# Window attention and a Mish feed-forward on one core: every engine's order from a list scheduler inside the kernel

## Chip, core and metric

The kernel runs on one core of a Trainium2 chip. TensorE (PE) multiplies matrices into PSUM, of which this kernel uses eight banks, VectorE (DVE), ScalarE (ACT) and GpSimd (POOL) work on tiles, and SyncE (SP) issues the transfers. The program gives each engine one queue of instructions; one that waits for another engine holds up those that stand behind it. The metric is the device time in microseconds of one execution.

## Reference

Windowed causal attention (window 64, 8 sequences of 576 tokens, 8 heads of 64), whose output is the input of a feed-forward 512 -> 2048 -> 512 with the Mish function between:

```python
scores = scale * np.matmul(q, k.transpose(0, 1, 3, 2))
scores = np.where(mask, scores, -1000000000.0)
attn = np.exp(scores - np.max(scores, axis=-1, keepdims=True))
attn = attn / (np.sum(attn, axis=-1, keepdims=True) + 1e-09)
x = np.matmul(attn, v)                      # then heads side by side: 4608 x 512
h = x @ w_in
g = h * np.tanh(np.log1p(np.exp(h)))        # Mish
out = g @ w_out
```

All is float32. The kernel multiplies in the format fp32r: each operand of the feed-forward is split into a high and a low part, and three products (high x high, high x low, low x high) are summed.

## The kernel before

**Tiling.** The 4608 tokens are cut into 12 chunks of 384. For each chunk, attention runs in four units, one for each pair of heads, and gives one of four 128-row blocks of x^T. Then the feed-forward runs in 16 steps, one for each block of 128 hidden values; step f of chunk c is written (c,f) here. A step is H: 12 matmuls into one of two h banks (four blocks of x, three products each), then Mish on ACT (L220), a high part gh (ACT L222 in chunk 0, POOL L224 later), a low part gl (POOL L225), and, two steps later (LAG = 2), A: 9 matmuls into the three accumulator banks of the chunk. The last A of a chunk is followed by a copy of each bank and a store (L241 to L244).

**A unit of attention** is S: scores (24 small matmuls on the profile); for each of six 128 x 128 tiles a masked row minimum on DVE (L149) and an exponential on ACT (L152); a normalisation on DVE (L156 to L162); a transposition; V: the product with v (24 small matmuls); and the split of x into xh (ACT L204) and xl (DVE L205). In chunks 0 to 3 the transposition is T: six PE transposes and two copies out of PSUM (L183, L184); from chunk 4 on DVE transposes 32 x 32 blocks and 12 small transfers move them (L172, L177).

**Weights.** The 16 blocks of weights arrive as 64-bit floats, one 1 MB transfer each (L251), and are converted in the kernel: absolute value on ACT (L261), four operations on DVE (L262, L264, L265, L266), the high part on ACT (L270), the low part on DVE (L271). A load waits until the weights three blocks earlier are converted (the lines on `used`). Weight f is needed by H and A of (0,f), and after that by every chunk.

**Order.** Chunk 0 runs eight steps alone, then its steps alternate with those of chunk 1, whose step f stands beside step f + 8 of chunk 0 (HEAD = 8). The four units of chunk 1 are spread over the first eight steps, those of chunk 2 over the last steps of chunk 1, and the units of every later chunk over the steps of the chunk before it. Up to the start of chunk 2 the tile framework's scheduler decides in which order each engine gets these instructions; it sees `high_priority` marks only. From chunk 2 on, `in_order` ties PE to the order of the program text. PSUM banks come from three pools (accumulators 3, h 2, attention 3), whose tiles are handed out as the text asks for them.

Of the kernel before, what the change touches and what calls it, by code (L numbers as in the profile page):

```python
# [13 lines left out]
I64 = mybir.dt.int64  # L14
# [8 lines left out]
SOON = 400  # L23
WP = 512


@with_exitstack
def tile_window_attn_mish_ffn(
# [13 lines left out]
    NC_ = NPAIR  # L42
# [6 lines left out]
    LAG = 2  # L49

    const = ctx.enter_context(tc.tile_pool(name="const", bufs=1))
    xp = ctx.enter_context(tc.tile_pool(name="xp", bufs=1))
    ap_ = ctx.enter_context(tc.tile_pool(name="ap_", bufs=2))
    mp = ctx.enter_context(tc.tile_pool(name="mp", bufs=2))
    ps_acc = ctx.enter_context(tc.tile_pool(name="ps_acc", bufs=1, space=bass.MemoryType.PSUM))
    ps_h = ctx.enter_context(tc.tile_pool(name="ps_h", bufs=2, space=bass.MemoryType.PSUM))
    ps_at = ctx.enter_context(tc.tile_pool(name="ps_at", bufs=3, space=bass.MemoryType.PSUM))

    nc.scalar.preload_act_table_set("exp_and_others")
    ident = const.tile([P, P], F32, name="ident")  # L60
    make_identity(nc, ident)

# [19 lines left out]
    ws = []  # L82


    pTs = [const.tile([P, P // 32, HM, 32], F32, name=f"pT{i}") for i in range(2)]
    for t in pTs:
        nc.gpsimd.memset(t, 0.0)
    pTs = itertools.cycle(pTs)


    order = []
    ordered = []

    def pe(*args, **kw):
        order.append(nc.tensor.matmul(*args, **kw).ins)  # L95
# [11 lines left out]
    def load_qk(c, p):  # L110
        q_t = ap_.tile([P, CH], F32, name="q_t")
        k_t = ap_.tile([P, CH + BLK], F32, name="k_t", bufs=2)
        parts = NM if c == 0 and p < 1 else 1
        for i in range(parts):
            a, b = i * CH // parts, (i + 1) * CH // parts
            nc.sync.dma_start(q_t[:, a:b], qT[p, :, c * CH + a:c * CH + b])
            a, b = a + BLK * (i > 0), b + BLK
            nc.sync.dma_start(k_t[:, a:b], kT[p, :, c * CH + a:c * CH + b])
        return q_t, k_t

    def load_v(c, p):

        v_t = ap_.tile([P, NB, P], F32, name="v_t", bufs=2)
        src = vN[p, c * CH:, :]
        nc.sync.dma_start(v_t, bass.AP(tensor=vN.tensor, offset=src.offset,
                                       ap=[[P, P], [BLK * P, NB], [1, P]]))
        return v_t

    def att_scores(c, p, tiles):
        q_t, k_t = tiles  # L130
        s_ps = [bank(c, p, "s_ps").rearrange("p (m k) -> p m k", k=P) for _ in range(2)]
        pr = ap_.tile([P, HM, P], F32, name="pr", bufs=2)
        mx = ap_.tile([P, HM], F32, name="mx", bufs=3)
        sm = ap_.tile([P, HM], F32, name="sm", bufs=3)
        for m in range(NM):
            for par, h in ((0, 0), (1, 1), (1, 0), (0, 1)):
                n = 2 * m + par
                rows = slice(h * BLK, (h + 1) * BLK)
                pe(s_ps[h][par * BLK:(par + 1) * BLK, m, :],
                   q_t[rows, n * BLK:(n + 1) * BLK], k_t[rows, n * BLK:n * BLK + P],  # L140
                                 start=True, stop=True)
        for h in range(2):
            js = slice(h * NM, (h + 1) * NM)
            for m in range(NM):
                first = [(c * NB + 2 * m + par) % blocks_per_seq == 0 for par in range(2)]
                mk = firsts[first.index(True)] if any(first) else mask
                j = h * NM + m

                nc.vector.tensor_tensor_reduce(  # L149
                    out=pr[:, j, :], in0=s_ps[h][:, m, :], in1=mk,  # L150
                    op0=ALU.add, op1=ALU.min, scale=-0.125, scalar=3.0e38, accum_out=mx[:, j:j + 1])
                nc.scalar.activation(pr[:, j, :], pr[:, j, :], AF.Exp, bias=mx[:, j:j + 1], scale=-1.0,  # L152
                                     accum_out=sm[:, j:j + 1])
            if c == 0:

                nc.vector.tensor_scalar(sm[:, js], sm[:, js], 1e-9, None, ALU.add)  # L156
                nc.vector.reciprocal(sm[:, js], sm[:, js])
                nc.vector.tensor_tensor(pr[:, js, :], pr[:, js, :], sm[:, js].unsqueeze(2).to_broadcast([P, NM, P]), ALU.mult)
        if c > 0:
            nc.vector.tensor_scalar(sm, sm, 1e-9, None, ALU.add)  # L160
            nc.vector.reciprocal(sm, sm)
            nc.vector.tensor_tensor(pr, pr, sm.unsqueeze(2).to_broadcast([P, HM, P]), ALU.mult)  # L162
        return pr

    def att_transpose(c, p, pr):
        pT = next(pTs)
        if c > 3:


            moved = []  # L170
            tr = ap_.tile([P, P // 32, HM, 32], F32, name="tr", tag="pr", bufs=2)
            nc.vector.transpose(tr.rearrange("p k j i -> p j k i"),  # L172
                                pr.rearrange("p j (k i) -> p j k i", i=32))
            for r in range(0, P, 32):
                for k in range(0, P, 32):
                    if 0 <= k - r % BLK <= BLK:
                        moved.append(nc.sync.dma_start(pT[k:k + 32, r // 32, :, :], tr[r:r + 32, k // 32, :, :]))  # L177
            return pT, moved
        for h in range(2):
            t_ps = (bank(c, p, "t_ps") if c else ps_h.tile([P, CH], F32, name="t_ps", tag="h_ps")  # L180
                    ).rearrange("p (m k) -> p m k", k=P)
            for m in range(NM):
                nc.tensor.transpose(t_ps[:, m, :], pr[:, h * NM + m, :], ident)  # L183
            (nc.scalar.copy if h == 0 or c == 1 else nc.vector.tensor_copy)(  # L184
                pT[:, :, h * NM:(h + 1) * NM, :].rearrange("p r m i -> p m r i"),
                t_ps.rearrange("p m (r i) -> p m r i", i=32))
        return pT, []

    def att_values(c, p, v_t, pT, x):
        pT, moved = pT  # L190
        xh, xl = x
        o_ps = bank(c, p, "o_ps")
        for n in range(NB):
            m, par = n // 2, n % 2
            for h in range(2):
# [237 lines left out]
```

## Time and profile before

| | |
|---|---|
| median of 3 runs | 979.98 us (979.28 to 980.83) |
| the profiled execution | 979.27 us, its span 977.5 us |
| mean granted TensorE clock | 0.976 |
| busy share of the span: PE / DVE / ACT / POOL | 95% / 28% / 43% / 30% |
| chain that ended last | PE 87%, DVE 7%, ACT 3% |
| matmuls of H: 2304, of A: 1728 | 81% of the chain is theirs (40% and 39% as the page rounds them) |

The span is the time from the first to the last instruction; the execution's own time is 1.77 us longer. The shares are averages over two quite different parts: the first eighth, in which weights are converted and PE has gaps, and the rest, in which PE has none. They must be read apart, which the prediction does.

### The profile page before, as it was taken

The page shows a single profiled execution, that of the slowest core. Times are in us where ns is not written, and L with a number is a line of the kernel's source. Part 1 is how long each engine was busy: PE and PEld are TensorE (multiplying, and loading weights), DVE is VectorE, ACT ScalarE, POOL GpSimd, SP SyncE. Part 2 cuts the span into 40 slices and gives each one's busy share as a digit, 9 for nine tenths or more (in the row PEclk, how much of TensorE's full clock was granted, in tenths as well). Part 3 has the DMA queues.
Part 4 walks back from the last instruction along what each step waited for, and adds up shares of the span by engine and source line. Part 5 has one row for each costly group of instructions (what it writes and reads, how often), then busy time and mean ns, then how long its engine had stood idle before and what let it go on. Part 6 is the DMA issues. An engine that isn't in the chain of part 4 may idle for free.

```text
span 977.5 us, 16844 instructions
## 1 busy us (share of the span) xinstructions
PE 929.9 (95%) x6432; PEld 821.7 (84%) x6432; DVE 276.3 (28%) x916; ACT 417.8 (43%) x1004; POOL 292.8 (30%) x385
## 2 busy tenths in 40 slices
PE   4698599998999999999999999999999999999998
PEld 2586399887888898888889888898888889889997
DVE  6988800122231321221221221221221221220000
ACT  5689511553553533533533443443443353451111
POOL 1023033231223233333333333333323323323332
PEclk9599699998999999999999999999999999999999
DMA  9655200122121311311311312322222221210000
GB/s 312 229 193 199 95 1 1 50 68 83 52 68 47 113 53 53 113 51 54 112 51 55 110 51 56 101 60 56 90 71 56 85 78 54 84 30 13 33 1 33
DMA packets 78033, 76.09 MB, mean 78 GB/s; under 512 B 9344, under 2 KB 71296, under 8 KB 75904
## 3 DMA queue, kind: packets, MB, share of 16 engines
q1 hardware_dynamic: 77952, 75.01, 24.5%
q8 instruction: 51, 0.84, 0.4%
q14 instruction: 30, 0.25, 0.1%
HBM read 56.10 MB, written 9.44 MB: 67 GB/s over the span
## 4 chain that ended last, share of the span: by engine, by line
PE 87%; DVE 7%; ACT 3%; issue 1%; DMA 1%; SPq 1%; ACTq 0%
PE h_ps L95 40%; PE acc L95 39%; PE o_ps L95 4%; PE s_ps L95 4%; DVE w L271 1%; DVE wa L265 1%; DVE wa L266 1%; DMA st<-w 1%; DVE wa L262 1%; DVE wa L264 1%; ACT wa L261 1%; ACT pr L152 1%; DVE pr L149 1%; PE t_ps L183 1%; ACT L220 1%
## 5 line engine op out<-in xcount | busy, mean ns | idle before, releaser
L95 PE MATMUL h_ps<-xh,w 128*128 128x384 f32 x1536 | 431.1, 341 | 3.7 <-ACT xh L204 2.7
L95 PE MATMUL acc<-w,gh 128*128 128x512 f32 x1152 | 363.5, 397 | 1.5 <-ACT gh L222 1.5
L95 PEld LDWEIGHTS h_ps<-xh,w 128*128 128x128 f32 x1536 | 284.2, 190 | 13.9 <-ACT xh L204 3.3
L220 ACT ACTIVATE t<-h_ps 128x384 f32<-128x384 f32 x192 | 94.0, 491 | 440.4 <-PE h_ps L95 439.7
L95 PE MATMUL h_ps<-xl,w 128*128 128x384 f32 x768 | 260.8, 340 | 2.9 <-DVE xl L205 2.9
L224 POOL TENSOR_SCALAR gh<-t 128x384 fp32r<-128x384 f32 x176 | 90.3, 513 | 568.6 <-ACT t L220 566.1
L95 PEld LDWEIGHTS acc<-w,gh 128*128 128x128 f32 x1152 | 211.9, 188 | 39.7 <-issue 6.3
L225 POOL TENSOR_TENSOR gl<-t,gh 128x384 fp32r<-128x384 f32 x192 | 198.4, 1034 | 106.9 <-ACT gh L222 92.2
L95 PE MATMUL acc<-w,gl 128*128 128x512 f32 x576 | 224.5, 391 | 0.6 <-POOL gl L225 0.6
L95 PEld LDWEIGHTS h_ps<-xl,w 128*128 128x128 f32 x768 | 145.8, 190 | 11.5 <-DVE xl L205 3.9
L205 DVE TENSOR_TENSOR xl<-o_ps,xh 128x384 fp32r<-128x384 f32 x48 | 26.7, 556 | 379.4 <-ACT xh L204 379.4
L95 PEld LDWEIGHTS acc<-w,gl 128*128 128x128 f32 x576 | 108.2, 188 | 25.1 <-POOL gl L225 1.0
L152 ACT ACTIVATE pr<-pr,mx 128x128 f32<-128x128 f32 x288 | 112.1, 391 | 14.8 <-DVE mx L149 14.3
L149 DVE CUSTOM_DVE_ANT_0 pr<-s_ps,mask 128x128 f32<-128x128 f32 x288 | 64.6, 285 | 30.8 <-PE s_ps L95 30.8
L220 ACT ACT_TABLE_LOAD x48 | 61.6, 1283 | 12.7 <-PE h_ps L95 12.4
L152 ACT ACT_TABLE_LOAD x42 | 53.9, 1283 | 28.9 <-DVE mx L149 28.7
L95 PEld LDWEIGHTS o_ps<-pT,v_t 128*64 128x64 f32 x1152 | 43.7, 150 | 24.3 <-issue 11.2
L95 PE MATMUL o_ps<-pT,v_t 128*64 128x64 f32 x1152 | 51.9, 240 | 9.8 <-DVE pT L184 4.7
L95 PE MATMUL s_ps<-k_t,q_t 64*64 64x128 f32 x1152 | 50.8, 293 | 4.0 <-DMA k_t<-kT 4.0
L152 ACT ACTIVATION_READ_ACCUMULATOR pr<-pr,mx 128x1 f32 x288 | 54.0, 187 | 0.0
L243 DVE COPY o<-acc 128x512 f32<-128x512 f32 x12 | 8.3, 692 | 149.2 <-PE acc L95 148.8
L95 PEld LDWEIGHTS s_ps<-k_t,q_t 64*64 64x64 f32 x1152 | 36.1, 140 | 11.3 <-DMA q_t<-qT 3.9
(36 smaller groups left out, 343.9 us busy)
## 6 DMA issues: line engine op xcount, KB each, us to landing
v_t<-vN SPq DMA_DIRECT2D x48, 384.0 KB, 3.7
st<-w SPq DMA_DIRECT2D x16, 1024.0 KB, 5.1
k_t<-kT SPq DMA_DIRECT2D x47, 224.0 KB, 3.8
out<-o SPq DMA_DIRECT2D x36, 256.0 KB, 2.1
pT<-tr SPq DMA_DIRECT2D x384, 24.0 KB, 1.8
q_t<-qT SPq DMA_DIRECT2D x47, 192.0 KB, 3.7
q_t<-qT SPq DMA_DIRECT2D x3, 64.0 KB, 2.0
k_t<-kT SPq DMA_DIRECT2D x2, 64.0 KB, 2.1
```

The lines of the kernel that those rows point to most:

```text
L95: order.append(nc.tensor.matmul(*args, **kw).ins)
L149: nc.vector.tensor_tensor_reduce(out=pr[:, j, :], in0=s_ps[h][:, m, :], in1=mk, op0=ALU.add, op1=ALU.min, scale=-0.125, scalar=3.0e38, acc ...
L152: nc.scalar.activation(pr[:, j, :], pr[:, j, :], AF.Exp, bias=mx[:, j:j + 1], scale=-1.0, accum_out=sm[:, j:j + 1])
L183: nc.tensor.transpose(t_ps[:, m, :], pr[:, h * NM + m, :], ident)
L205: nc.vector.tensor_tensor(xl[:, p, :], o_ps, xh[:, p, :].bitcast(F32), ALU.subtract)
L220: nc.scalar.activation(t, h_ps, AF.Mish)
L224: nc.gpsimd.tensor_scalar(gh, t, 1.0, 0.0, ALU.mult, ALU.add)
L225: nc.gpsimd.tensor_tensor(gl, t, gh.bitcast(F32), ALU.subtract)
L261: nc.scalar.activation(af, hi.bitcast(F32), AF.Abs)
L262: nc.vector.tensor_scalar(af, af, BIG, TINY, ALU.min, ALU.max)
L264: nc.vector.tensor_scalar(a, a, 3, 0x3FFFFFFF, ALU.logical_shift_left, ALU.bitwise_and)
L265: nc.vector.scalar_tensor_tensor(a, hi, 0xC0000000, a, ALU.bitwise_and, ALU.bitwise_or)
```

## The change

All pools and the framework's scheduling go. Every tile and PSUM bank is named by hand (rings of fixed buffers; accumulators A, attention banks B, two h banks H), every piece of work becomes a task with an engine, a cost, a rank and the tasks that it waits for, and a list scheduler in the kernel (`Plan.order`) plays the program once with the table of costs and issues the tasks in the order in which it started them. Wherever an engine is free it takes, of the tasks that are ready at that moment, the one of lowest rank (a change of ACT's function table adds 50 to a rank).

What else differs:

- Chunk 1 follows chunk 0 by seven steps (TRAIL = 7), and the ranks put its first unit (unit 4) next to the units of chunk 0.
- Weights get ranks behind the units of chunk 0. A load waits for the conversion two blocks earlier, not three. From block 5 on the absolute value is taken on DVE.
- In chunks 0 and 1, gh is made on ACT and gl on DVE; POOL makes both from chunk 2 on.
- Accumulators of chunk 0 are A, of chunk 1 B, of later ones A; units of chunk 2 use A after chunk 0 has been stored. They run during the last seven steps of chunk 1.
- Chunk 3 is transposed by DVE and transfers, as later chunks were.
- q and k of the first unit come as one transfer each (before: three each), k on ACT's queue.
- DVE copies two of the three output banks, ACT one (before: the other way round).
- H of the first two steps of chunk 0 is cut into four tasks, so that it can begin before the last block of x; the first and last A of a chunk are cut by bank.

```diff
+COST = {
+    "h": 2.08, "hcc": 0.52, "acc": 2.06, "acc1": 0.687, "scores": 0.85, "values": 0.88, "tr": 0.65,
...
+SLOW_UNTIL, SLOW = 70.0, 1.2
...
+            now = [rt for rt in ready[e] if rt[0] <= at + 1e-6]
+            pick = min(now, key=key)
...
+            free[e] = t.start + t.cost * (SLOW if e == "PE" and at < SLOW_UNTIL else 1.0)
...
+        return sorted(self.tasks, key=lambda t: (t.start, t.n))
...
+    ctx.enter_context(tc.manual_schedule())
...
+        pace = used[f - 2:f - 1] if f > 1 else []
...
+        load = add("SP", "issue", load, writes=[buf], rank=rank - 1.5, size=P * 2 * WP * 8,
+                   after=pace or [units[f].scored])
+        if on_act:
+            x = add("ACT", "abs", lambda: nc.scalar.activation(af, words[1].bitcast(F32), AF.Abs),
+                    reads=[buf], writes=[abuf], rank=rank, table="exp")
+        else:
+            x = add("DVE", "absv", lambda: nc.vector.tensor_scalar(a, words[1], 0x7FFFFFFF, None, ALU.bitwise_and),
+                    reads=[buf], writes=[abuf], rank=rank)
...
+        queue = nc.scalar if c == 0 and p == 0 else nc.sync
...
+        post = -1 + rank * 1e-3 if c < 2 else rank - 6
...
+        if c < 2:
+            add("ACT", "gh", lambda: nc.scalar.copy(gh, t), reads=[tb], writes=[ghb], rank=post)
+            add("DVE", "gl", lambda: nc.vector.tensor_tensor(gl, t, gh.bitcast(F32), ALU.subtract),
+                reads=[tb, ghb], writes=[glb], rank=post)
...
+    RANK_U = [0, 1, 4, 6, 2, 21, 34, 36]
...
+    RANK_U += [140 + i for i in range(4)]
...
+    def r_ffn(c, f):
+        return 100 + 10 * f + (TRAIL * 10 + 5 if c else 0)
...
+    seq = sorted([(f + TRAIL * c + 0.5 * c, c, f) for c in range(2) for f in range(NF)])
+    for n, (_, c, f) in enumerate(seq):
+        ffn_in(c, f, r_ffn(c, f), False, c == 0 and f < 2)
...
+    tasks = plan.order()
...
+    for t in tasks:
+        t.emit()
```

What this does to the order shows at three places.

**DVE, the last unit of chunk 0.** Before, ahead of `xl`, the low part of the last block of x of chunk 0 (the last row below), DVE's order holds six weights all but finished; this is the end of that stretch. L149 is the masked minimum of unit 4, `wa` the weights under conversion, `w` their low part, `st` the loaded words.

```order
L149 ISA pr,mx<-s_ps,mask 128x128
L149 ISA mx 128x1
L264 TENSOR_SCALAR wa<-wa 128x1024
L271 TENSOR_TENSOR w<-wa,w 128x2x512
L265 SCALAR_TENSOR_TENSOR wa<-st,wa 128x1024
L160 TENSOR_SCALAR sm<-sm 128x6
L205 TENSOR_TENSOR xl_233<-o_ps,xh_232 128x384
```

Now the same instruction (L398, the last row) has only the first weight finished ahead of it and the second begun.

```order
L327 TENSOR_TENSOR pr_95<-pr_95,sm_101 128x768
L248 TENSOR_SCALAR wa_119<-wa_119 128x1024
L353 COPY pT_104<-acc_125 128x3x4x32
L266 TENSOR_TENSOR w<-wa_118,w 128x2x512
L249 TENSOR_SCALAR wa_119<-wa_119 128x1024
L314 ISA pr_96,mx_99<-at_129,mask 128x128
L314 ISA mx_99 128x1
L251 SCALAR_TENSOR_TENSOR wa_119<-st,wa_119 128x1024
L398 TENSOR_TENSOR xl_121<-acc_126,xh_120 128x384
```

In all, before holds 28 operations on weights ahead of that row (six each of L262, L264 and L265, five each of L266 and L271), now eight (two each of L248, L249, L251, one each of L256, L266); the first row of the second fence is the normalisation of unit 4, which before comes later.

**PE, the first unit of chunk 1.** `acc`, `at`, `h` are banks; `k_t,q_t` marks scores, `pT,v_t` values, `xh` and `xl` H, `gh` and `gl` A. Before, the values of unit 4 stand inside H of (0,4), with the scores of unit 5 between them:

```order
L95 MATMUL h_ps<-xh_232,w 128x384
L95 MATMUL o_ps<-pT_102,v_t 64x64
L95 MATMUL s_ps<-k_t,q_t 64x128 x12
L95 MATMUL o_ps<-pT_102,v_t 64x64 x11
L95 MATMUL h_ps<-xh_232,w 128x384
```

Now they stand right behind the first two banks of A of (0,0), ahead of H of (0,1), which begins in the last row:

```order
L295 MATMUL at_129<-k_t_91,q_t_89 64x128
L451 MATMUL acc_124<-w,gh_109 128x512 x2
L451 MATMUL acc_124<-w,gl_112 128x512
L451 MATMUL acc_125<-w,gh_109 128x512 x2
L451 MATMUL acc_125<-w,gl_112 128x512
L384 MATMUL at_127<-pT_103,v_t_93 64x64 x12
L409 MATMUL h_130<-xh_120,w 128x384
```

The scores in the first of these rows are already those of unit 6, which before come behind H of (0,8). All four units of chunk 1 are now done ahead of H of (0,6); before, the values of the last one come behind H of (0,9).

**ACT, the units of chunk 2.** Before, exponentials (L152) and Mish (L220) share ACT in groups of three to six and one or two:

```order
L152 ACT_TABLE_LOAD
L152 ACTIVATE pr,sm<-pr,mx 128x128 x6
L204 CAST xh_1681<-o_ps 128x384
L220 ACT_TABLE_LOAD
L220 ACTIVATE t<-h_ps 128x384 x2
L184 COPY pT_102<-t_ps 128x3x4x32
```

Now (L318 exponential, L424 Mish, L426 gh):

```order
L424 ACT_TABLE_LOAD
L424 ACTIVATE t_106<-h_130 128x384
L318 ACT_TABLE_LOAD
L318 ACTIVATE pr_95,sm_101<-pr_95,mx_98 128x128
L426 CAST gh_111<-t_106 128x384
L353 COPY pT_104<-acc_126 128x3x4x32
L318 ACTIVATE pr_95,sm_101<-pr_95,mx_98 128x128 x2
L424 ACT_TABLE_LOAD
L424 ACTIVATE t_107<-h_131 128x384
```

Each Mish now stands alone between two table loads, and gh is ACT's too: from the first exponential of the four units to the Mish behind the last there are 12 loads, before ten.

More of the change, by code (lines that the diff above doesn't have):

```diff
@@ L121, in load_v @@
-    def load_v(c, p):
-        v_t = ap_.tile([P, NB, P], F32, name="v_t", bufs=2)
-        src = vN[p, c * CH:, :]
[L125 to L134, printed above, removed]
+    ident = const.tile([P, P], F32, name="ident")
@@ L138, in att_scores @@
                 rows = slice(h * BLK, (h + 1) * BLK)
-                pe(s_ps[h][par * BLK:(par + 1) * BLK, m, :],
-                   q_t[rows, n * BLK:(n + 1) * BLK], k_t[rows, n * BLK:n * BLK + P],
+                nc.tensor.matmul(u.s[h][0][par * BLK:(par + 1) * BLK, m * P:(m + 1) * P],
+                                 u.q[0][rows, n * BLK:(n + 1) * BLK], u.k[0][rows, n * BLK:n * BLK + P],
                                  start=True, stop=True)
-        for h in range(2):
[L143 to L158, printed above, removed]
@@ L193, in att_values, with emit_values @@
+    def emit_values(u):
+        v_t, pT, o_ps = u.v[0], u.pT[0], u.o[0]
         for n in range(NB):
@@ L196, in att_values @@
                 rows = slice(h * BLK, (h + 1) * BLK)
-                pe(o_ps[rows, n * BLK:(n + 1) * BLK], v_t[:, n, rows],
-                   pT[:, 2 * par:2 * par + 2, h * NM + m, :], start=True, stop=True)
-                for d in moved:
-                    tc.add_manual_dep(order[-1], d.ins.name, SYNC, reason="values in one piece")
-                moved = []
-        with tc.high_priority(offset=SOON):
-            nc.scalar.copy(xh[:, p, :], o_ps)
-            nc.vector.tensor_tensor(xl[:, p, :], o_ps, xh[:, p, :].bitcast(F32), ALU.subtract)
@@ L395, in tile_window_attn_mish_ffn, with values @@
-    while pend:
-        with in_order():
-            flush()
+                mm = nc.tensor.matmul(o_ps[rows, n * BLK:(n + 1) * BLK], v_t[:, n, rows],
+                                      pT[:, 2 * par:2 * par + 2, h * NM + m, :], start=True, stop=True)
+                for d in u.moved:
+                    tc.add_manual_dep(mm.ins, d.ins.name, SYNC, reason="values in one piece")
+                u.moved = []
+    def values(u, rank, chain):
+        add("PE", "values", lambda: emit_values(u), reads=[u.v[1], u.pT[1]], writes=[u.o[1]], rank=rank, chain=chain)
@@ new lines, in tile_window_attn_mish_ffn, with bank, tail, front @@
+    rot = [0]
+    def bank(pool):
+        rot[0] += 1
+        return pool[(rot[0] - 1) % 3]
+    def tail(i):
+        u, r = units[i], RANK_U[i]
+        if i >= 4:
+            pool = B if i < 8 else A
+            u.t = [bank(pool), bank(pool)]
+            u.o = bank(pool)
+        turn_pe(u, r, ("ACT", "ACT") if 4 <= i < 8 else ("ACT", "DVE"), False)
+        values(u, r, False)
+        refill_v(i)
+        x_parts(u, r)
+    def front(i):
+        u, r = units[i], RANK_U[i]
+        if i >= 4:
+            pool = B if i < 8 else A
+            u.s = [bank(pool), bank(pool)]
+        scores(u, r, False)
+        refill_qk(i)
+        softmax(u, r, i < 4)
@@ new lines, in tile_window_attn_mish_ffn @@
+    for n, (c, f) in enumerate(steps):
+        r = 1000 + 10 * n
+        ffn_in(c, f, r, True, False)
+        for kind, i in sorted(runs.get(n, []), key=lambda x: x[0], reverse=True):
+            u = units[i]
+            if kind == "s":
+                u.s, u.o = B[:2], B[2]
+                scores(u, r, True)
+                refill_qk(i)
+                softmax(u, r - 4, False)
+                turn_dma(u, r - 4)
+            else:
+                values(u, r, True)
+                refill_v(i)
+                x_parts(u, r - 5)
+        if n >= LAG:
+            ffn_out(*steps[n - LAG], r + 15, True)
```

577 lines of the change are left out of this document (357 added, 220 removed).

## Prediction

> **What bounds the kernel now.** The page's slices and a table of windows come first: they say where PE, which carries 87% of the chain, is not at work. The columns of a window are its length, then busy time and count for PE, PEld (weight load), DVE, ACT and POOL, the granted clock, the DMA share and GB/s.
>
> ```profile
> PE   4698599998999999999999999999999999999998
> DVE  6988800122231321221221221221221221220000
> PEclk9599699998999999999999999999999999999999
> 0.00:49.10 49.10, 27.19 (x260) 20.08 (x260) 41.56 (x122) 29.75 (x82) 4.12 (x17) 0.76 0.79 271
> 49.10:121.60 72.50, 54.95 (x385) 45.37 (x385) 64.66 (x103) 58.11 (x101) 13.36 (x9) 0.90 0.47 163
> 121.60:223.10 101.50, 101.47 (x627) 89.60 (x627) 12.88 (x63) 37.88 (x88) 31.37 (x39) 0.99 0.09 29
> 223.10:235.50 12.40, 9.07 (x53) 8.20 (x52) 2.87 (x6) 4.25 (x11) 0.15 (x1) 0.72 0.33 98
> 235.50:977.50 742.00, 737.17 (x5110) 658.45 (x5109) 154.38 (x623) 287.80 (x725) 243.76 (x320) 1.00 0.21 63
> ```
>
> Up to 121.6 us PE is busy 27.2 + 55.0 = 82.1 us and idle 39.5, while DVE is busy 106.2: softmax and weights on DVE bound this stretch. From 121.6 to 223.1 PE has no gap; from 223.1 to 235.5 it loses 3.3 us waiting for the last unit of chunk 2; from there it is busy 737.2 of 742.0 us, the rest being the last copy and store. So the change can win only ahead of 235.5. The pitch of PE's work, from the chain (start, length, what) and the timeline (the same, by runs of instructions):
>
> ```profile
> 160.71 2.11 PE h_ps L95 x12
> 164.87 2.11 PE h_ps L95 x12
> 334.52 0.92 PE L95 MATMUL o_ps<-pT,v_t 128*64 128x64 f32 x24
> 353.05 0.92 PE L95 MATMUL o_ps<-pT,v_t 128*64 128x64 f32 x24
> 205.62 0.87 PE L183 MATMUL t_ps<-ident,pr 128*128 128x128 f32 x6
> 206.42 0.65 PE L95 MATMUL s_ps<-k_t,q_t 64*64 64x128 f32 x6
> ```
>
> H to H is 4.16 us, a **step** (H 2.1, A 2.06). Two V in a row start 18.53 us apart with four steps and one S + V between, so S + V cost 18.53 - 16.64 = 1.89. T costs 0.80. The first two chunks' 32 steps and the first three chunks' 12 units are then 133.1 + 12 x 2.69 = 165.4 us of PE at full rate. Before spends 235.5 on them.
>
> **The part behind chunk 1.** At 235.5 before still has A of (1,15) to do and has done H of (2,0); these cancel. The time behind chunk 1's last A is then 742.0 us, less the four T of chunk 3, which leave PE for DVE and transfers: 742.0 - 3.2 = 738.8. I cost nothing for their new path: scores and values of a chunk-3 unit stand four steps apart, as in later chunks, whose window shows no gap. The last copy on DVE instead of ACT is worth a tenth. With T1 for the end of chunk 1's last A, span = T1 + 738.8.
>
> **When the feed-forward gets under way.** Before, `xl` of the last block of x of chunk 0 releases PE. Below it stand DVE operations by start and length; the step from one start to the next is what an operation costs the queue.
>
> ```profile
> 48.54 0.55 DVE L205 TENSOR_TENSOR xl<-o_ps,xh 128x384 fp32r<-128x384 f32 x1
> 49.14 0.45 PE L95 MATMUL h_ps<-xl,w 128*128 128x384 f32 x1 [0.82 <-DVE xl L205]
> 49.00 1.22 DVE L266 SCALAR_TENSOR_TENSOR wa<-st,wa 128x1024 uint32<-128x1024 uint32 x1
> 50.14 0.69 DVE L262 TENSOR_SCALAR wa<-wa 128x1024 f32<-128x1024 f32 x1
> 50.74 0.18 DVE L161 RECIPROCAL sm<-sm 128x6 f32<-128x6 f32 x1
> 50.86 0.69 DVE L264 TENSOR_SCALAR wa<-wa 128x1024 uint32<-128x1024 uint32 x1
> 51.47 0.95 DVE L162 TENSOR_TENSOR pr<-pr,sm 128x768 f32<-128x768 f32 x1
> 52.34 1.22 DVE L271 TENSOR_TENSOR w<-wa,w 128x1024 fp32r<-128x1024 f32 x1
> 61.66 1.22 DVE L271 TENSOR_TENSOR w<-wa,w 128x1024 fp32r<-128x1024 f32 x1
> 62.79 1.22 DVE L266 SCALAR_TENSOR_TENSOR wa<-st,wa 128x1024 uint32<-128x1024 uint32 x1
> 12.53 0.28 DVE L149 CUSTOM_DVE_ANT_0 pr<-s_ps,mask 128x128 f32<-128x128 f32 x1
> 12.74 0.28 DVE L149 CUSTOM_DVE_ANT_0 pr<-s_ps,mask 128x128 f32<-128x128 f32 x1
> ```
>
> A short weight operation (L262, L264) costs 0.61, a long one (L265, L266, L271) 1.13, a six-tile normalisation 0.87, `xl` 0.46, a masked minimum 0.21. By the order, before has 12 short and 16 long weight operations ahead of this `xl`, 25.4 us; now 4 and 4, 7.0: 18.4 us less. Unit 4's normalisation with its two small operations (0.87 + 0.3) and one more minimum (0.2) now stand ahead: +1.4. DVE was busy 41.6 of the 49.1 us, so nearly all of this counts: 49.1 - 18.4 + 1.4 = 32.1.
>
> ```profile
> q_t<-qT SPq DMA_DIRECT2D x47, 192.0 KB, 3.7
> q_t<-qT SPq DMA_DIRECT2D x3, 64.0 KB, 2.0
> st<-w SPq DMA_DIRECT2D x16, 1024.0 KB, 5.1
> ```
>
> The first q lands whole after 3.7 us, not in thirds after 2.0, and k is issued behind ACT's first table load; the thirds overlapped with scores, so I take 1.2 us of the 1.7: 33.3. Last, weights no longer fill DVE's waits in the softmax of chunk 0. If all of them stay filled, 33.3 holds or 32 with an unchanged first load; if the 7.5 us in which DVE idled there come once more, 41. I take a third of that, **36**, since scores of units 4 and 5 still fill some.
>
> By then PE has done units 0 to 3 (10.8), scores of units 4 and 5 and half a T (2.2), and three quarters of H of (0,0) (1.6): 165.4 - 14.6 = **150.8** remain.
>
> **What holds PE up after that.** Three terms.
>
> ```profile
> 229.25 4.14 PE h_ps L95 x12
> 18.04 1.22 DVE L271 TENSOR_TENSOR w<-wa,w 128x1024 fp32r<-128x1024 f32 x1
> 118.69 1.23 DVE L271 TENSOR_TENSOR w<-wa,w 128x1024 fp32r<-128x1024 f32 x1 [1.17 <-ACT w L270]
> L270 ACT CAST w<-wa 128x1024 fp32r<-128x1024 f32 x16 | 16.7, 1046 | 8.1 <-DVE wa L266 8.0
> 17.00 1.56 PE L95 MATMUL s_ps<-k_t,q_t 64*64 64x128 f32 x24
> ```
>
> (a) Clock: after a gap H took 4.14 us instead of 2.11. One such start is **2** us (0 if the units keep the clock up, 4 if a second gap follows).
>
> (b) Weights. DVE's share of one weight is now 3 short operations (the absolute value, taken like L264, for which before has no row on DVE) and 3 long, 5.2 us, plus two gl. Before has no gl on DVE; the nearest row is `xl`, the same subtraction at 0.46. That makes 6.1 us for each weight against 8.3 for two steps of PE, so once both chunks run PE is the slower, and the later gl and absolute values cost nothing: PE hides them, and would pay about 2 us for each 2 us by which DVE went over 8.3. Before the units of chunk 1 are done it is the other way round: (0,1) to (0,5) need five weights (26 us), three units (six minima, normalisation, `xl`, 2.9 us each) and four gl (2), 37 us of DVE, against five steps and three units of PE, 29 us. DVE does some of this before 36, the first weights being under way. I take **5** us of waiting, between 2 (one Mish, gh, gl chain ahead of A of (0,0)) and 12, most of the 17.5 us that PE idled in before's second window. A load now waits for the weight two back, and behind it on SP stand loads of q, k and v; landing takes 5.1 us, less than the 6.1 of one weight, so nothing comes late for it.
>
> (c) The units of chunk 2, in the last seven steps of chunk 1, share ACT with Mish and gh.
>
> ```profile
> 190.21 0.49 ACT L220 ACTIVATE t<-h_ps 128x384 f32<-128x384 f32 x1
> 190.72 1.28 ACT L152 ACT_TABLE_LOAD   x1
> 192.01 0.40 ACT L152 ACTIVATE pr<-pr,mx 128x128 f32<-128x128 f32 x1
> L152 ACT ACTIVATE pr<-pr,mx 128x128 f32<-128x128 f32 x24 | 9.3, 390 | 3.4 <-DVE mx L149 3.4
> 221.41 0.87 PE L95 MATMUL s_ps<-k_t,q_t 64*64 64x128 f32 x12
> 226.22 0.85 PE L183 MATMUL t_ps<-ident,pr 128*128 128x128 f32 x6 [3.08 <-DVE pr L162]
> ```
>
> Twelve loads are 15.4 us, 24 exponentials 9.4, six Mish and six gh (taken alike) 6, eight copies out of PSUM (taken alike) 4: 35 us of ACT beside 6 H, 6.7 A and four units on PE, 37 us. ACT just fits. Between the last scores and their transposes before had 226.2 - 222.3 = 3.9 us of chain, 3.1 of it idle on PE; now A, T, H, V and A stand there, 8 us, which covers it. I take **3** us, between 0 and 8 (a Mish held up by a load and a few exponentials in each of four units).
>
> The Trainium skill, "ScalarE: Activation LUTs", section "What ACT_TABLE_LOAD costs", puts a switch at about 1283 ns of load and 1380 ns of drain. The trace agrees with the first and shows no second: Mish ends at 190.70, the load runs 190.72 to 192.00, the exponential starts at 192.01. By that section ACT would need 16.6 us more for the twelve.
>
> **Sum.** T1 = 36 + 150.8 + 2 + 5 + 3 = 196.8; span 935.6; the profiled execution lies 1.77 us above its span and 0.7 below the median of the runs: 938.1 against 979.98. All low ends give T1 = 184.8 and 926, all high ends 215.8 and 957.
>
> **Rivals.**
> 1. *The fixed order waits where the list did not expect it.* The planner puts scores in this stretch at 0.85 x 1.2 = 1.02 us; at low clock before shows 24 of them in 1.56 us (17.00 above). If what then stands first in a queue is late, all behind it is. If PE idles as it did from 49.1 to 121.6 (17.5 us instead of 5) and x comes 2 us later, T1 = 211.3, time 952.6. For it: DVE's stretch up to (0,5) has no slack. Against: PE and DVE had such orders before, and the gap came from chunk 1's x arriving after the weights.
> 2. *ACT limits the end of chunk 1.* If a switch held ACT for a load and as long again, about 16 us more, T1 would grow by 13: 951. The rows above speak against it.
> 3. *Slower: weights one after another.* Should a load and its conversion not overlap, a weight takes 5.1 + 5.2 + 1.0 (high part on ACT) = 11.3 us. With the first at 31 the last comes at 31 + 15 x 11.3 = 200.5; behind it stand half a step, eight steps and chunk 2's units, 46 us: T1 = 246.5, time 987.8. It turns slower than before at T1 = 238.7, 10.8 us for each weight. Against: before's first and last L271 are 100.6 us apart, 6.7 for each of 15, with units between, and two loads may be under way.
> 4. *More than forecast*, below 927: DVE's waits all filled and weights just in time.
>
> **How the numbers follow.** Forecast 0.64, rival 1 0.20, rival 2 0.03, rival 3 0.05, rival 4 0.08. Predicted is the forecast, 938.1. From 927 to 956 lie the forecast with nearly all its bounds and rivals 1 and 2. A measurement of this kernel tells about 0.2% from no change: slower is rival 3 alone (0.05), same a chance meeting near its turning point (0.01), faster the rest (0.94).
>
> **What would show it.** Right: the last `xl` of chunk 0 near 36 us; PE's idle time up to its last A of chunk 1 mostly ahead of 36; no PE gap from about 70 us to 160; chunk 1's last A near 197; 739 us from there to the end; no T in chunk 3. Wrong: `xl` beyond 41 (DVE's waits were hidden by weights), H waiting for L266 in step after step (weights set the pace), H or A waiting for ACT from 160 on, or gaps behind chunk 2's start, which the whole sum takes as unchanged.

## The result and the profile after

The changed kernel takes 939.51 us (median of four runs, 937.72 to 940.72), against 979.63 of the kernel before in runs on the same chip: a ratio of 0.959 (95% interval 0.957 to 0.961), 40 us less. The execution that was profiled took 938.71 us, 1.8 above its span of 936.9.

Of the page of the changed kernel, the rows of busy tenths in 40 slices:

```profile
PE   6789999999999999999999999999999999999998
DVE  5999952433232122212222123113212222220000
PEclk9799999999999999999999999999999999999999
```

Before, the slices of PE dip in the first five and again at the tenth. Now only the first three (and the last) are under 9, and the granted clock is under 9 tenths in one slice instead of three. The table of windows, with the columns of before (length, busy time and count of PE, PEld, DVE, ACT and POOL, clock, DMA share, GB/s):

```profile
0.00:33.90 33.90, 22.70 (x273) 17.48 (x274) 24.35 (x106) 21.18 (x76) 4.22 (x17) 0.92 0.81 256
33.90:80.00 46.10, 40.53 (x312) 33.88 (x311) 45.89 (x94) 36.70 (x76) 0.00 (x0) 0.95 0.58 201
80.00:157.30 77.30, 77.30 (x388) 69.66 (x386) 52.31 (x67) 28.92 (x48) 0.00 (x0) 1.00 0.28 101
157.30:194.80 37.50, 37.50 (x353) 32.33 (x353) 18.41 (x75) 33.32 (x80) 0.00 (x0) 1.00 0.30 91
194.80:936.90 742.10, 738.04 (x5089) 656.22 (x5087) 163.49 (x634) 281.17 (x710) 243.94 (x320) 1.00 0.22 65
```

Up to chunk 1's last A at 194.8 us PE is idle 11.2 + 5.6 = 16.8 us; before, up to 235.5, it was 21.9 + 17.6 + 0 + 3.3 = 42.8. That is 26.0 us less idle time. The same work also kept PE busy for 178.0 us instead of 192.7, at a clock of 0.92 and 0.95 in the first two windows, where before had 0.76, 0.90 and 0.72 in three of its four. 26.0 + 14.7 = 40.7 us is what T1, the end of chunk 1's last A, has gained. Nothing was gained behind it: that part takes 742.1 us, where 738.8 was forecast and before had 742.0.

The two rows that mark T1 and the release of the feed-forward, from the timelines of DVE and PE (start, length, what):

```profile
33.42 0.55 DVE L398 TENSOR_TENSOR xl<-acc,xh 128x384 fp32r<-128x384 f32 x1
194.53 0.39 PE L451 MATMUL at<-w,gl 128*128 128x512 f32 x1
194.76 0.34 PE L409 MATMUL h<-xh,w 128*128 128x384 f32 x1
```

The last `xl` of chunk 0 ends at 34.0 us, and the first H of chunk 2 starts at 194.76, right behind the last A of chunk 1. What PE waited for between 34 and 157 us, the four longest groups (waits by line: total, times, longest):

```profile
PE at L348 <- DVE mx L314: 2.1, 2, 1.1
PE acc L451 <- DVE gl L427: 1.5, 2, 0.8
PE at L348 <- DVE pr L327: 0.8, 1, 0.8
PE at L295 <- ACT pT L353: 0.6, 1, 0.6
```

All of it lies ahead of 73 us. Of the 5.6 us that PE waits, 4.4 are for DVE, which is busy 45.9 of the 46.1 us from 33.9 to 80.

### The profile page after: what moved, and what is told of

It is laid out like the page before. It is cut to its first block, busy times and chain, and to the rows that moved or that the text cites. A ratio compares the mean times of both kernels' runs of the same rounds, so it can differ in the third digit from the quotient of the medians.

```text
span 936.9 us, 16721 instructions
## 1 busy us (share of the span) xinstructions
PE 916.1 (98%) x6408; PEld 809.6 (86%) x6408; DVE 304.4 (32%) x971; ACT 401.3 (43%) x989; POOL 248.2 (26%) x337
## 4 chain that ended last, share of the span: by engine, by line
PE 92%; DVE 5%; DMA 1%; issue 0%; ACT 0%; SPq 0%
PE h L409 42%; PE acc L451 39%; PE at L451 4%; PE at L384 3%; PE at L295 3%; DVE wa L251 1%; DVE wa L256 1%; DMA st<-w 1%; DVE w L266 1%; DVE pr L314 1%; DVE pr L327 1%; PE acc L295 1%; DVE wa L248 0%; DMA k_t<-kT 0%; PE acc L384 0%
## 5 line engine op out<-in xcount | busy, mean ns | idle before, releaser
L409 PE MATMUL h<-xh,w 128*128 128x384 f32 x1536 | 426.2, 338 | 0.0
L409 PEld LDWEIGHTS h<-xh,w 128*128 128x128 f32 x1536 | 281.7, 188 | 8.4 <-issue 0.3
L424 ACT ACTIVATE t<-h 128x384 f32<-128x384 f32 x192 | 94.2, 491 | 430.4 <-PE h L409 429.8
L409 PE MATMUL h<-xl,w 128*128 128x384 f32 x768 | 258.5, 337 | 0.0
L432 POOL TENSOR_TENSOR gl<-t,gh 128x384 fp32r<-128x384 f32 x160 | 162.0, 1013 | 13.3
L409 PEld LDWEIGHTS h<-xl,w 128*128 128x128 f32 x768 | 144.6, 188 | 7.8
L398 DVE TENSOR_TENSOR xl<-at,xh 128x384 fp32r<-128x384 f32 x41 | 22.8, 557 | 335.7 <-ACT xh L397 335.7
L318 ACT ACTIVATE pr<-pr,mx 128x128 f32<-128x128 f32 x288 | 112.2, 391 | 9.5 <-DVE mx L314 8.9
L314 DVE CUSTOM_DVE_ANT_0 pr<-at,mask 128x128 f32<-128x128 f32 x252 | 57.0, 285 | 22.2 <-PE at L295 22.2
L318 ACT ACTIVATION_READ_ACCUMULATOR pr<-pr,mx 128x1 f32 x288 | 54.0, 187 | 0.0
L327 DVE TENSOR_TENSOR pr<-pr,sm 128x768 f32<-128x768 f32 (+1 forms) x52 | 46.4, 895 | 1.4
L295 PE MATMUL at<-k_t,q_t 64*64 64x128 f32 x1008 | 40.2, 287 | 2.4 <-DMA k_t<-kT 1.1
L384 PE MATMUL at<-pT,v_t 128*64 128x64 f32 x984 | 38.0, 226 | 1.0 <-ACT pT L353 0.4
```

The lines of the kernel that those rows point to most:

```text
L295: nc.tensor.matmul(u.s[h][0][par * BLK:(par + 1) * BLK, m * P:(m + 1) * P], u.q[0][rows, n * BLK:(n + 1) * BLK], u.k[0][rows, n * BLK:n * ...
L314: x = add("DVE", "ttr", lambda: nc.vector.tensor_tensor_reduce(out=pr[:, j, :], in0=u.s[h][0][:, m * P:(m + 1) * P], in1=mk, op0=ALU.add, ...
L318: return add("ACT", "exp", lambda: nc.scalar.activation(pr[:, j, :], pr[:, j, :], AF.Exp, bias=mx[:, j:j + 1], scale=-1.0, accum_out=sm[:, ...
L327: return add("DVE", "norm3" if n == NM else "norm6", lambda: nc.vector.tensor_tensor(pr[:, js, :], pr[:, js, :], sm[:, js].unsqueeze(2).to ...
L384: mm = nc.tensor.matmul(o_ps[rows, n * BLK:(n + 1) * BLK], v_t[:, n, rows], pT[:, 2 * par:2 * par + 2, h * NM + m, :], start=True, stop=True)
L398: add("DVE", "xl", lambda: nc.vector.tensor_tensor(xl[:, p, :], o_ps[:, :CH], xh[:, p, :].bitcast(F32), ALU.subtract), reads=[u.o[1]], wri ...
```

## The experiments

Two questions were open. **Which part of the change carries the gain?** The theory was the prediction's: the weights now stand behind the softmax of chunk 0 on DVE, x is ready early, and once both chunks run PE has no gap. The rivals were the early unit 4, gl's move from POOL to DVE, and the distance of seven steps. **Why are there 742.1 us behind T1 and not 738.8?** No PE wait is there and no T in chunk 3, but two V in a row stand 18.62 us apart in the changed kernel, where before had 18.53:

```profile
482.22 0.92 PE L384 MATMUL at<-pT,v_t 128*64 128x64 f32 x24
500.84 0.92 PE L384 MATMUL at<-pT,v_t 128*64 128x64 f32 x24
```

### Both kernels again, on one chip

No edit.

> The kernel before, unchanged, profiled on the same chip as the changed one. The part behind chunk 1's last A took 742.1 us in the changed kernel where 738.8 was forecast, since a step of its steady part took 4.185 us against 4.16 before. If the two kernels' code or tiles make the difference, two V in a row with four steps and one S between them stand 18.53 us apart here, and 18.62 in the changed kernel on the same chip. If it was the chip or the execution, both show the same pitch, 18.53 or 18.62.

> The changed kernel, unchanged, on the same chip as the kernel before. Kernel as the cause: a pitch of 18.62 us (two V in a row) and 742 us from the last A of chunk 1 to the end. Chip or execution as the cause: the pitch of the kernel before on this chip, and 739 us. Last xl of chunk 0 ends at 34 us and chunk 1's last A at 195 us either way.

On the same chip, in one execution each, the kernel before took 981.1 us with its V at 483.97 and 502.50 us, 18.53 apart. The changed kernel took 940.16, with V at 483.58 and 502.20, 18.62 apart, and 741.9 us behind T1. So the longer step belongs to the kernel, not to the chip. T1 came at 196.4 us in this execution instead of 194.8: between these two executions of one kernel the start differs by 1.6 us, the steady part by 0.2.

### The tiles in other places

```
...
-    gh_ring = Ring("gh", 3, [P, CH], F32R)
+    gh_ring = Ring("gh", 3, [P, CH], F32R, space=mp)
...
-    xs = [[const.tile([P, NPAIR, CH], F32R, name=f"x{n}{i}") for n in "hl"] for i in range(2)]
+    xs = [[xp.tile([P, NPAIR, CH], F32R, name=f"x{n}{i}") for n in "hl"] for i in range(2)]
```

> The changed kernel with its SBUF tiles in four pools in the order of the kernel before (constants and weights, then x, then q, k, v, pr, then the feed-forward's), so that x, gh, gl and the weights lie where they lay or near it; no instruction is another. If the places of the tiles make a step 0.025 us longer, the pitch falls from 18.62 to 18.53 us and the time by 3 us to 936.5. If something else does, the pitch stays at 18.62 and the time at 939.5 within 1.

Measured: 935.56 us (ratio 0.954, interval 0.953 to 0.956), V 18.53 us apart, 738.8 us behind T1. No instruction was changed, and the missing 3.3 us are back: the places of the tiles had cost them. What about the places it was, the next three runs show.

### 64 bytes

In the changed kernel all tiles lie in one pool in the order of their declaration. The six tiles `mx` and `sm` take 32 bytes each, 192 together, so all tiles behind them (pT, t, gh, gl, o, wa, x, w) start 64 bytes off a multiple of 128. In the kernel before, w and x lie in pools ahead of `mx` and `sm`, at a multiple of 128, while gh and gl lie behind them, 64 off.

```
+    const.tile([P, 16], F32, name="pad")
     xs = [[const.tile([P, NPAIR, CH], F32R, name=f"x{n}{i}") for n in "hl"] for i in range(2)]
```

> The changed kernel with 64 bytes of each partition left empty ahead of x: x and the weights move up by 64 bytes and then start at a multiple of 128, as they did before and in the run with the tiles in four pools; in the changed kernel they start 64 bytes off one. Nothing else moves. If the 64 bytes make a step 0.025 us longer, two V in a row stand 18.53 us apart, 738.8 us lie behind chunk 1's last A, and the time falls by 3 to 4 us to about 936. If it is which tiles lie beside which, the pitch stays at 18.62 and the time within 1 us of 940.

Measured: 935.94 us (ratio 0.955, interval 0.953 to 0.956), 738.9 us behind T1, and in the timeline of this run V stand 18.53 us apart:

```profile
481.03 0.92 PE L385 MATMUL at<-pT,v_t 128*64 128x64 f32 x24
499.56 0.92 PE L385 MATMUL at<-pT,v_t 128*64 128x64 f32 x24
```

> The changed kernel with t, gh, gl, o and wa in a pool behind the weights, so that x and the weights move down by 29,696 bytes but still start 64 bytes off a multiple of 128, while Mish's and POOL's tiles now lie on the other side of the weights, as before. If the 64 bytes are the cause, the pitch stays at 18.62 us and 742 us lie behind chunk 1's last A. If the neighbourhood of the tiles is the cause, 18.53 and 738.8.

The edit of this run is the one on gh_ring above, for t, gh, gl, o and wa alone. Measured: 939.08 us (one execution), V at 482.49 and 501.11, 18.62 apart, 741.9 us behind T1. The neighbourhood of the tiles does nothing, as expected if the 64 bytes are the cause. The last run of this question moved the same empty tile one place up, ahead of pT:

```
+    const.tile([P, 16], F32, name="pad")
     pT_ring = Ring("pT", 2, [P, P // 32, HM, 32])
```

> The changed kernel with the 64 empty bytes one place earlier, ahead of pT: not only x and the weights, but also t, gh, gl, o and wa then start at a multiple of 128 (in both kernels and in every run so far they start 64 off one). If the 64 bytes cost PE on any operand, the nine weight loads of gh and gl in each step gain what the ones of x and w gained: up to 0.025 us a step, 160 steps behind chunk 1's last A and 32 ahead, 4 to 5 us, time 931 to 932. If DVE's and ACT's operations on wa and t also go faster, the long weight operation falls below 1.22 us and T1 falls too. If only x or the weights count, the pitch is that of the run with the 64 bytes ahead of x, 18.53 us, and the time 936 within 1.

Measured: 940.51 us (ratio 0.960, interval 0.958 to 0.961), V at 484.84 and 503.46, 18.62 apart. **This expectation failed, and with it the rule behind the earlier two**: w and x start at a multiple of 128 here, and the step is long all the same. What the runs have in common shows in A's matmuls from 300 to 900 us (by one line of the program: count, then shortest/median/longest in ns). The changed kernel, where w and gl both start 64 bytes off:

```profile
L451 PE MATMUL acc<-w,gl x391: 389/397/398, 299.6 to 899.3; 128*128 128x512 f32 x196
```

The run with 64 bytes ahead of x (w at a multiple of 128, gl 64 off):

```profile
L452 PE MATMUL acc<-w,gl x392: 388/388/398, 302.2 to 899.5; 128*128 128x512 f32 x196
```

The run with t, gh, gl, o and wa last (both 64 off):

```profile
L452 PE MATMUL acc<-w,gl x391: 389/397/398, 299.9 to 899.5; 128*128 128x512 f32 x196
```

The run with all at a multiple of 128:

```profile
L452 PE MATMUL acc<-w,gl x390: 389/397/398, 300.9 to 897.7; 128*128 128x512 f32 x195
```

The median is 397 ns where gl, the operand that is loaded, and w, the one that streams, start at the same place modulo 128, and 388 where they start 64 bytes apart. The run with other places (w at a multiple of 128, gl 64 off) has 388 too, and the kernel before (the same) 389. Matmuls overlap, so what a step costs is read from one start to the next, worked out from the same traces (medians): the nine matmuls of an A take 2.081 us in the changed kernel, in the run with t, gh, gl, o and wa last and in the run with all at a multiple of 128, and 2.061 in the other three; the twelve of an H take 2.105 or 2.106 in all six. That is 20 ns a step, 0.08 us in four steps and 3.2 us in the 160 behind T1, as measured (742.1 against 738.9). The medians leave out that about three H in ten differ as well (2.110 us against 2.084). The longer gl matmul stays so from 85 to 155 us, where POOL is idle (means of 396 in the changed kernel, 388 with the 64 bytes), so POOL is not the other party. In all six placements x lies with w, and t, gh, o and wa lie with gl, modulo 128: that it is gl and w, and not another pair of these tiles, follows only from the matmul in which it shows. The Trainium skill, "SBUF — State Buffer", section "Who interferes with whom", gives PE two independent read ports, one for the operand that streams and one for the loaded one, and says that PE waits on nobody; here the measured times differ with the place of these two operands. Why the matmul with gl is slowed and those with gh are not, no run tells.

### The weights first

```
-    RANK_W = [15, 18, 5, 30, 16, 14] + [55 + 5 * i for i in range(10)]
+    RANK_W = [-4, -3, -2, -1, 16, 14] + [55 + 5 * i for i in range(10)]
```

> The changed kernel with the first four weights ranked ahead of the softmax of chunk 0, as they stood before: 13 short and 15 long weight operations (24.9 us of DVE) ahead of the last xl of chunk 0 instead of 4 and 4 (7.0). Theory (x of chunk 0 is early because the weights stand behind it): this xl moves from 34 us to between 42 (weights fill the 9.6 us in which DVE idled) and 52 (all 17.9 count), about 47 us; PE's 5.6 us of waits behind it go in part, since the weights are ready then, so T1 rises by 7 to 13 us, to about 204, and the time to about 949. Rival (the gain comes from unit 4 being early and from gl off POOL, not from the weights' place): xl may move but the time stays within 3 us of 939.5.

Measured: 952.4 us (ratio 0.971, interval 0.970 to 0.973), 12.9 us above the changed kernel. From DVE's timeline and the windows:

```profile
50.10 0.55 DVE L398 TENSOR_TENSOR xl<-acc,xh 128x384 fp32r<-128x384 f32 x1
0.00:50.60 50.60, 27.62 (x286) 20.75 (x286) 42.19 (x124) 27.10 (x80) 4.24 (x17) 0.78 0.69 233
50.60:80.00 29.40, 26.62 (x212) 21.91 (x212) 25.47 (x68) 25.30 (x62) 0.00 (x0) 0.86 0.62 210
```

`xl` ends at 50.65 instead of 33.97: 16.7 of the 17.9 us of added operations count. DVE was idle 8.4 of the 50.6 us, against 9.5 of 33.9, so weights hardly fill its waits for scores and exponentials. Behind `xl` PE makes up little: T1 is 208.6, 13.8 us later, where 7 to 13 were expected. The mechanism of the prediction holds, at the high end of what was expected. The rival, that the weights' place is worth under 3 us, falls.

### Unit 4 late

```
-    RANK_U = [0, 1, 4, 6, 2, 21, 34, 36]
+    RANK_U = [0, 1, 4, 6, 20, 21, 34, 36]
```

> The changed kernel with the first unit of chunk 1 ranked 20 instead of 2, ahead of the second one only. Theory (the place of the weights carries the gain, DVE's sum decides): five minima and a normalisation (2 us) leave the queue ahead of the last xl of chunk 0, one long weight operation (1.1) comes in, so xl ends at 33; the same 2 us come back in the stretch up to 73 us, where DVE is busy without a break, so T1 rises by 0 to 2.5 us and the time is 940 to 942. Rival (the early unit is what keeps PE from waiting for chunk 1): PE waits in the stretch up to 80 us grow by the 5 us or more that a unit's softmax lasts, time 945 or more.

Measured: 941.31 us (ratio 0.960, interval 0.959 to 0.962), 1.8 above the changed kernel, with `xl` at 32.8 and T1 at 196.84. The longest wait of PE behind `xl`, from its timeline:

```profile
48.41 1.53 PE L384 MATMUL at<-pT,v_t 128*64 128x64 f32 x22 [3.05 <-ACT pT L353]
```

The values of unit 4 now wait, but what they lose, DVE had gained ahead of 33 us. The time lies in the theory's range and far from the rival's. The effect itself is not shown: 1.8 us is about what T1 differed by between two executions of the changed kernel (1.6), and the two intervals overlap.

### One weight at a time

```
-        pace = used[f - 2:f - 1] if f > 1 else []
+        pace = used[f - 1:f] if f > 0 else []
```

> The changed kernel with each weight's load held back until the weight ahead of it (not two ahead) has had its low bits added. A weight then takes 5.0 us of landing and 4.1 of DVE up to that point, 9.1 us, one behind the other. Theory (the weights' chain then sets the pace, as in the prediction's third rival, at a lower price): weight 15 is ready near 31 + 15 x 9.1 = 168 us, half a step, eight steps and chunk 2's units (46 us) stand behind it, T1 = 214 and the time about 958. By the full price of that rival, 11.3 us for each weight, T1 = 246 and 988. If the loads are hidden either way (PE needs a weight only every 8.3 us), T1 moves by under 3 us and the time stays below 943.

Measured: 972.55 us (ratio 0.992, interval 0.990 to 0.994), T1 at 227.28. One weight of this run, in the timeline of DVE, ACT and SP's queue, from the low bits of one to those of the next, with the first and the last such row of all 16 weights:

```profile
26.67 1.18 DVE L256 SCALAR_TENSOR_TENSOR wa<-st,wa 128x1024 uint32<-128x1024 uint32 x1
...
81.58 1.22 DVE L256 SCALAR_TENSOR_TENSOR wa<-st,wa 128x1024 uint32<-128x1024 uint32 x1
82.83 20.89 SPq L234 DMA_DIRECT2D st<-w  x3
...
87.63 0.70 DVE L246 TENSOR_SCALAR wa<-st 128x1024 uint32<-128x1024 uint32 x1 [2.49 <-DMA st<-w]
88.36 0.69 DVE L248 TENSOR_SCALAR wa<-wa 128x1024 f32<-128x1024 f32 x1
89.41 0.56 DVE L427 TENSOR_TENSOR gl<-t,gh 128x384 fp32r<-128x384 f32 x1 [0.36 <-ACT gh L426]
...
90.61 1.23 DVE L251 SCALAR_TENSOR_TENSOR wa<-st,wa 128x1024 uint32<-128x1024 uint32 x1
91.87 1.23 DVE L256 SCALAR_TENSOR_TENSOR wa<-st,wa 128x1024 uint32<-128x1024 uint32 x1
...
182.19 1.23 DVE L256 SCALAR_TENSOR_TENSOR wa<-st,wa 128x1024 uint32<-128x1024 uint32 x1
```

The load (L234) starts when the low bits (L256) end and lands 4.8 us later; five operations, one behind the other, and a gl among them follow. From 26.67 to 182.19 us there are 15 such turns, (182.19 - 26.67) / 15 = 10.4 us each. The expectation had 9.1: an operation that waits for the one before it takes 0.73 or 1.26 us from start to start, not the 0.61 or 1.13 of independent ones, and gl comes in between with 0.8. The time lies between the two that were expected, 958 and 988. The weights set the pace, as the third rival said, and the time comes close to before's. Two loads under way are what keeps that rival from happening.

### gl on POOL

This and the next two runs have the 64 empty bytes, and are compared with 935.94 us.

```
-            add("DVE", "gl", lambda: nc.vector.tensor_tensor(gl, t, gh.bitcast(F32), ALU.subtract),
+            add("POOL", "poolgl", lambda: nc.gpsimd.tensor_tensor(gl, t, gh.bitcast(F32), ALU.subtract),
```

> The run with the 64 empty bytes, with gl of the first two chunks on POOL again as before the change. Theory (DVE, busy 45.4 of the 46.1 us from 34 to 80 us, sets that stretch): five or six gl of 0.47 us leave DVE there, 2.5 us less; but while POOL ran gl in the kernel before, a long weight operation of DVE took 2.0 us instead of 1.2, so each gl hands back about 0.8: T1 moves by -2.5 (POOL disturbs nothing) to +3 us (every gl meets a long operation), and the time is 934 to 939; gl itself is ready later, since POOL takes about 1.0 for it. Rival (moving gl off POOL carried a good part of the change's gain): the time rises by 5 us or more, to 941 or above.

Measured: 944.18 us (ratio 0.963, interval 0.961 to 0.964), 8.2 more. The theory's range is missed and the rival holds. Groups of instructions from 80 to 157 us (shapes, count, busy time, mean ns) of this run:

```profile
L252 DVE SCALAR_TENSOR_TENSOR wa<-st,wa 128x1024 uint32<-128x1024 uint32 x8 | 13.2, 1654 | 0.2
L250 DVE TENSOR_SCALAR wa<-wa 128x1024 uint32<-128x1024 uint32 x7 | 9.7, 1391 | 0.0
L428 POOL TENSOR_TENSOR gl<-t,gh 128x384 fp32r<-128x384 f32 x18 | 21.4, 1200 | 60.0 <-ACT gh L427 60.0
```

And of the run with gl on DVE:

```profile
L252 DVE SCALAR_TENSOR_TENSOR wa<-st,wa 128x1024 uint32<-128x1024 uint32 x8 | 9.8, 1223 | 0.2
L250 DVE TENSOR_SCALAR wa<-wa 128x1024 uint32<-128x1024 uint32 x7 | 4.8, 689 | 0.1
L428 DVE TENSOR_TENSOR gl<-t,gh 128x384 fp32r<-128x384 f32 x19 | 10.5, 554 | 18.7 <-ACT gh L427 18.7
```

While POOL does 18 gl, L252 takes 1654 ns instead of 1223 and L250 1391 instead of 689: 8 x 0.43 + 7 x 0.70 = 8.4 us more on DVE, 0.46 for each gl. That is as much as a gl costs on DVE itself (0.46 to the next start), so DVE is relieved of nothing, while gl is ready after 1.2 us instead of 0.55. From 33.9 us to the first H of chunk 2 (203.1, before 194.7) PE is idle 12.0 us instead of 7.1, now in 80 to 157 us too, and busy 3.6 us longer for the same work; together that is the 8.4 us by which this H starts later. The same section of the Trainium skill's "SBUF — State Buffer" says that a DVE instruction with two SBUF inputs contends with a GpSimd instruction that reads SBUF, and that a DVE instruction in a mode with two ports and a GpSimd instruction block each other for a whole instruction. The trace agrees for L252, which has two inputs; L250 has one, and no run shows its mode. L257 has two inputs and keeps its length (1225 ns against 1222), but no gl of POOL runs beside it in this stretch.

### Four steps behind

```
-    TRAIL = 7
+    TRAIL = 4
```

> The run with the 64 empty bytes, with chunk 1 four steps behind chunk 0 instead of seven. The order up to 75 us is the same; chunk 2's four units now stand among two H and four A instead of five and seven, the last two with next to nothing between their scores, transposes and values. Theory (the seven steps are what covers the softmax of chunk 2): the last unit's transposes wait about 2 us (3.9 us of chain after its scores less T and V), the last values about 1 each for the copies out of PSUM, so T1 rises by 3 to 6 us and the time to 939 to 942. Rival (ACT or the chain is fast enough, the trail is worth nothing): within 1 us of 936.

Measured: 946.63 us (ratio 0.966, interval 0.964 to 0.967), 10.7 more. The units of chunk 2 in PE's timeline, and the window around them:

```profile
191.68 0.88 PE L349 MATMUL acc<-ident,pr 128*128 128x128 f32 x6 [0.75 <-DVE pr L328]
193.38 0.92 PE L385 MATMUL acc<-pT,v_t 128*64 128x64 f32 x24 [0.82 <-ACT pT L354]
196.05 1.17 PE L349 MATMUL acc<-ident,pr 128*128 128x128 f32 x6 [0.94 <-DVE xl L399]
200.51 1.54 PE L349 MATMUL acc<-ident,pr 128*128 128x128 f32 x6 [1.72 <-DVE pr L328]
```

```profile
186.00:204.30 18.30, 13.43 (x177) 10.07 (x175) 10.90 (x42) 11.01 (x43) 0.00 (x0) 0.89 0.51 155
204.30:212.00 7.70, 7.70 (x37) 7.70 (x38) 0.56 (x1) 2.72 (x4) 2.85 (x4) 0.81 0.18 53
```

With next to no steps left between the units, PE waits for softmax and copies as expected: 18.3 - 13.4 = 4.9 us from 186 to 204.3. The measured 10.7 us lie well above the 3 to 6 that were expected, since the expectation had no clock in it: it is granted at 0.89 among the gaps and at 0.81 behind them, and the same work takes 3.6 us more up to the first H of chunk 2 (at 204.17 us) and 1.6 behind it. With 1.1 us of waits more ahead of 80 us that is, but for rounding, the 11.1 us by which the span is longer. The last transposes take 1.54 us, where the first in these rows take 0.88. Against four steps, the seven of the change are worth these 11 us.

### Chunk 3 transposed on PE

```
-                turn_dma(u, r - 4)
+                if i >= 16:
+                    turn_dma(u, r - 4)
...
+                units[i].t = B[:2]
+                turn_pe(units[i], r + 16, ("ACT", "DVE"), True)
```

> The run with the 64 empty bytes, with the four units of chunk 3 transposed on PE again, six transposes and two copies each, one step after their scores, instead of through DVE and 16-KB-and-more transfers between tiles. By the sum, four T of 0.80 us come back behind chunk 1's last A: 738.9 + 3.2 = 742.1 us, time 939.2. If a T also breaks the pitch or waits for softmax, up to 2 us more. If the transfers had cost PE something of their own, less than 3.2 comes back and the time stays below 938.

Measured: 938.22 us (ratio 0.957, interval 0.956 to 0.959), 2.3 more, with 741.1 us behind T1. The first T of chunk 3 and the H behind it:

```profile
212.30 0.82 PE L349 MATMUL at<-ident,pr 128*128 128x128 f32 x6
212.87 0.42 PE L410 MATMUL h<-xh,w 128*128 128x384 f32 x1
```

A T among steps takes 0.57 us, not 0.80, so four of them 2.3 instead of 3.2. The kernel before shows the same in chunk 3:

```profile
270.14 0.82 PE L183 MATMUL t_ps<-ident,pr 128*128 128x128 f32 x6
270.72 0.42 PE L95 MATMUL h_ps<-xh,w 128*128 128x384 f32 x1
```

The 0.80 of the prediction was read from a T (at 205.62 us) with scores behind it, where those of chunk 3 have H or A behind them.

## Why the prediction came out right

Forecast were 938.1 us, measured 939.51, and 938.71 in the execution that was profiled. The mechanism held: the gain lies ahead of T1, by an earlier release and shorter waits for DVE. That the total is so close is partly luck: T1 came 2.0 us earlier than forecast, and the part behind it took 3.3 us longer.

- **The release of the feed-forward.** Forecast 36, measured 33.97. The sum of the rows without waits had 33.3, and 0.7 more came: of the 2.7 us added for waits that weights no longer fill, 2.0 were too much. The weights-first run says why: 16.7 of 17.9 us count, so weights fill little of these waits where they stand ahead.
- **150.8 us of PE work at full rate, and the clock (a).** PE was busy 155.3 us from there to T1, 4.5 more. A clock of 0.95 over 46.1 us makes 2.3 of them, where (a) had 2; the longer step makes up to 0.7. The rest is not taken apart.
- **The weights (b).** Forecast 5 us of waits, measured 5.6, 4.4 of them for DVE as named. From 73 us on PE has no gap. The prediction had gl on DVE as a cost alone; the run with gl on POOL shows that the move saves 8.2 us, since POOL's gl would lengthen the weights' operations.
- **ACT in chunk 2's units (c).** Forecast 3, measured 0: PE is busy 37.50 of 37.50 us while ACT is busy 33.3. So rival 2 did not come. A switch with a drain, as the Trainium skill has it in "ScalarE: Activation LUTs", section "What ACT_TABLE_LOAD costs", would have needed 16.6 us more of ACT by estimate, where 4.2 were free; the trace shows no drain. The run with four steps shows what these waits cost where the steps are missing.
- **T1.** Forecast 196.8, measured 194.8. The 2 us are those of the first term; behind it 3 us too much for (c) stand against 2.5 too little for clock and work and 0.6 for (b).
- **738.8 us behind T1.** This is the step that failed: 742.1. The prediction took before's 742.0 as it stood, though the change also moved all tiles. The 64 bytes give it back (738.9 and 738.8 in two runs). The term in it for four T was too large as well, 3.2 against 2.3, since it was read from a T ahead of scores. 742.0 - 2.3 = 739.7 leaves 0.8 us to the measured 738.9. Of these, 0.5 lie behind the last matmul: from its end to the end of the span it is 4.4 us before and 3.9 in the run with the 64 bytes, where the prediction had a tenth for the last copy.
- **Rivals.** An order that waits (rival 1) would have had 17.5 us of waits; there were 5.6. Rival 3 put a weight at 11.3 us, and needed 10.8 to come out slower than before. One load at a time gave 10.4, and 972.55 us: this rival's price was near the truth, its condition was not met.

Single edits took back 12.9 us (weights first), 8.2 (gl) and 1.8 (unit 4, about what T1 varies): 23 of the 40.7 us that T1 gained, if they add up, which was not tried. The 2.3 us of T in chunk 3 lie behind T1. The other 18 us, the order that the list chose behind `xl` among them, are not taken apart by any run. Four steps instead of seven would cost 10.7 more, but before had neither.

The best version is the changed kernel with x and the weights 64 bytes further on (935.94 us) or with its tiles in four pools (935.56). Both intervals lie below that of the change as it was made.

## What to carry to other kernels

Where one engine is the bound over the whole, look for what releases its first dense stretch, and count every operation that stands ahead of that release on the engine that feeds it. Do not count on moved work to fill the waits between those operations: here DVE idled 9.5 us with the weights behind the softmax and 8.4 with them ahead. A gap on PE can cost more than its length: in the run with four steps 5.9 us more of gaps came with 5.2 us more of PE time for the same work, at a granted clock of 0.89 and 0.81. A change that rewrites the allocation moves every tile, so compare the mean length of the same matmul before and after even where no wait is seen.

## What was not expected of the hardware

- A matmul of 128x512 with gl as the loaded operand takes 397 ns in the median where gl and w start at the same place modulo 128 bytes, and 388 or 389 where they lie 64 apart, in all six placements that were looked at: that of before, that of the change and four others. An A then takes 2.081 us instead of 2.061, which over 160 steps makes 3.2 us of 939. The mechanism is open.
- POOL's gl takes as much from DVE as it saves it: 0.46 us for each, through L250 (one input, from 689 to 1391 ns) even more than through L252 (from 1223 to 1654).
- T costs 0.57 or 0.58 us to the next start where H or A stands behind it (four times in the run with chunk 3 on PE, and four times in chunk 3 of the kernel before). The one at 205.62 us of the kernel before, with scores behind it, took 0.80; whether the scores are the reason was not tried.
